# The second product of the last two local chunks in seven-product form for all eight blocks

## The chip, the cores and the metric

The kernel runs on one core of one Trainium2 chip. The metric is device time in microseconds (us) for one execution. A core has five engines that work side by side: TensorE (PE, matrix products), VectorE (DVE), ScalarE (ACT), GpSimd (POOL) and SyncE (SP, which here issues transfers). PE's weight loads are listed apart, as PEld.

## The reference

Eight batches of attention, each with 32 global and 512 local tokens and 8 heads of 64, give a matrix x of 8 x 544 = 4352 rows (one for each token) and 512 columns; two products with a cosine between them follow:

```python
h = x @ w_in                     # 4352 x 512 times 512 x 2048
g = h * np.cos(h)
return (g @ w_out).astype(np.float32)   # w_out: 2048 x 512
```

In the attention every local query sees the 32 global keys and the local keys at a distance of at most 32, and every global query sees all keys.

## The kernel before

**Numbers.** Values are f32. Each operand of a large product is split into two f16 parts, a high and a low one (names end in h and l), and a product is made of three matmuls: high by high, high by low, low by high.

**Tiling.** The tokens are cut into 17 chunks of 256: chunks 0 to 15 are local tokens, two for each batch, and chunk 16 (`NC`) holds the global tokens of all batches. A chunk passes through 8 blocks j, each of 256 of the 2048 columns of w_in. Attention of batch b runs interleaved with the chunks of the batch before, and ends at about 777 us; the chunks after that stand alone. For each block:

- `m1_a` (L1432): 24 matmuls of 256 columns, into the PSUM tile `ph`.
- `m1_b` (ACT L1449, DVE L1450) and `m1_c` (ACT sine, L774): the argument and the cosine, in tile `u`.
- `m1_d`: DVE multiplies (`gf`, L1467), ACT makes the high part (`gh`, L1478), POOL the low part (`gl`, L1479).
- the second product, into two PSUM tiles `po`. In the plain form, `m2_a` (L1585 to L1587), it is 12 matmuls of 512 columns. In the seven-product form it is a 2 x 2 block product after Winograd's scheme: 7 products of a quarter of the size in place of 8. `sv_a` runs four of them (12 matmuls of 256 columns) and `sv_y` three (9 matmuls of 256 columns), all through `three` (L1530). It needs sums of g's quarters, which are made in `m1_d` (four DVE operations on 128x128, L1474 to L1477, with their parts `ygh` on ACT, L1487, and `ygl` on POOL, L1488), and sums of w_out's quarters, which `w_sums` (L1498 to L1513) makes once for each j, around 210 to 250 us.

`seven(c, j)` says which blocks take the seven-product form: those with j of 0 or 1 in chunks 4 to 16, 26 blocks in all. `sv_copy` (L1558, L1560) takes the four quarters of `po` out of PSUM, `m2_b` (L1595, L1605) adds or scales the rest, and `m2_c` (L1622) sends it out.

**Order.** The body lists steps by slot (`at(slot, phase, function, ...)`); `slot0(c)` is the first slot of a chunk. What finally sets the order on each engine is the table `ORDER` (lines 21 to 290): for each engine a list of words `step.instruction`, from which every instruction gets a dependency on the one ahead of it in the table. No engine is free to take another order.

**Names at a place that the change moves.** In attention, `kl` (L917, on DVE) is the low part of a pair's scaled keys and queries, from `qkr` and its high part `qa` (L916, on ACT); `qk_e` moves halves of kh, qa and kl by transfers on SP's queue (L928 to L933), and PE's score matmuls (`ps`, L1184, L1185) need them. `sc_e` copies weights on ACT (`plx`, L1235), takes their low part on POOL (L1237), and a transposing transfer (L1242, `ptb<-plx`) brings them to `av_a` (L1274). `v_q` ends with `vm` (L486) and a PE transpose `pm_v` (L855).

Of the kernel before, what the change touches and what calls it, by code (L numbers as in the profile page):

```python
# [8 lines left out]
F16 = mybir.dt.float16  # L9
# [13 lines left out]
        18x4 22x4 23.4 23.0 23.5 23.1x2 23.6 23.3 23.7 27x4 29.4x3 29.0 29.7 29.1x3 33 33.2 33.1 33.3 35  # L23
        35.4 35.1x3 35.5x3 28x8 34x8 40 40.4 40.1 40.5 40.2 40.6x2 40.3 57 49 69x4 39x8 41x8 74 74.2
        74.1 74.3 64x24 67x24 72x24 108 108.2 108.1 108.3 91x24 106x24 125x24 109 109.4 109.1 109.5
        109.2 109.6 109.3 109.7 135x24 110x2 110.4 110.2 110.5x2 110.3 110.7 124 112x8 113x8 127 127.2
        127.1 127.3 141 141.4x4 141.1x3 143x24 149x8 150 150.4 150.1 150.5 150.2 150.6 150.3 150.7 164x3
        155x5 151x8 152x8 156x20 157x8 164 189x5 164x19 189x3 170x3 170.4 170.3 164 176x22 171x2 189x4
        176x2 187x2 171x18 195x4 196 196.2 196.1 196.3 187x22 206x24 208.6 208.0 208.7 208.1x2 208.8x2
        208.3 208.10 208.4 208.11 208.5 204 209x4 210 210.2 210.1 210.3 227x24 229x2 229.6x2 229.2 229.8  # L30
        229.3x3 229.9x3 250 250.6x3 250.1x2 250.9x2 250.3x3 250.11 274 274.6 274.1x3 274.7x2 274.4 274.9
        274.5 274.10x2 288.6 288.0 288.7 288.1x3 288.8x4 288.4x2 230x18 231x3 231.4x4 231.3 233 233.2
        233.1 233.3 300x2 300.6x3 300.2x2 300.9 300.4x2 300.10 248x24 272x21 234 234.2 234.1 234.3
        230x18 300 303.6 303.0x3 303.7x3 303.3x3 303.10x2 251x2 252x4 272x3 311x12 251x2 253x4 251x32
# [257 lines left out]
P = 128  # L292
# [6 lines left out]
DM = 512  # L299
# [38 lines left out]
T0 = [3, 1]  # L338
# [1576 lines left out]
```

## Time and profile before

| | us |
|---|---|
| median of 3 runs | 927.91 |
| lowest and highest | 926.1, 930.22 |
| the profiled execution's own time | 926.53 |
| its span in the trace | 924.7 |
| PE busy in the span | 876.5 (95%) |
| ACT, DVE, POOL busy | 707.6, 633.4, 511.3 |

The span runs from the first instruction to the last; the 1.8 us between span and time lie outside of it. PE's matmuls are pipelined: the duration printed for one of them is its latency, and what it costs is the distance from its start to the next one's start. The chain of work that ended last, followed back from the end, lies on PE for 56% of the span, on ACT, DVE and POOL for 11% each, and on transfers for 5%.

### The profile page before, as it was taken

How to read it: one execution, taken by the hardware profiler on the slowest of the kernel's cores; microseconds unless marked ns; L12 is line 12 of the kernel's file. 1: busy time of each engine (PE TensorE's matmuls, PEld its weight loads, DVE VectorE, ACT ScalarE, POOL GpSimd, SP SyncE). 2: the span in 40 equal slices, each digit the busy share in tenths (PEclk: the TensorE clock that was granted, in tenths of full speed). 3: DMA queues.
4: the chain of work that ended last, by engine and by line, in shares of the span. 5: the costliest groups of instructions: out<-in, count | busy, mean ns of one | idle time of the engine just before them, and what ended most of it. 6: DMA issues, size and time to landing. Idle time of an engine off the chain costs nothing.

```text
span 924.7 us, 21457 instructions
## 1 busy us (share of the span) xinstructions
PE 876.5 (95%) x8126; PEld 634.2 (69%) x8126; DVE 633.4 (68%) x1684; ACT 707.6 (77%) x1400; POOL 511.3 (55%) x765
## 2 busy tenths in 40 slices
PE   4879888999979999999999999999999999999997
PEld 3668645576756786767777776768686868686853
DVE  6998857599877887787679666778766645451520
ACT  5789998789969889888789798978888856453440
POOL 2577799736727656646565455565655554320340
PEclk9799999999999999999999999999999999999999
DMA  9774516876467666464566654573532524000000
GB/s 359 279 272 162 167 24 148 163 197 153 93 142 146 140 146 113 114 162 92 101 138 157 137 102 102 130 185 77 133 69 51 110 47 84 1 24 1 24 24 23
DMA packets 162423, 110.80 MB, mean 120 GB/s; under 512 B 140176, under 2 KB 142608, under 8 KB 160400
## 3 DMA queue, kind: packets, MB, share of 16 engines
q1 hardware_dynamic: 162176, 109.31, 48.6%
q8 instruction: 63, 1.03, 0.5%
q14 instruction: 40, 0.33, 0.1%
q10 hardware_dynamic: 144, 0.13, 0.1%
HBM read 51.61 MB, written 8.91 MB: 65 GB/s over the span
## 4 chain that ended last, share of the span: by engine, by line
PE 56%; ACT 11%; DVE 11%; POOL 11%; DMA 5%; issue 4%; SPq 1%; DVEq 0%; POOLq 0%; ACTq 0%
PE ph L1432 23%; PE po L1587 7%; PE po L1585 7%; PE po L1586 7%; PE po L1530 4%; DMA ptb<-plx 3%; ACT t L774 2%; PE acc L1274 2%; ACT L774 2%; POOL t L1230 2%; POOL gl L1479 2%; POOL plx L1237 2%; DVE kl L917 1%; POOL plx L819 1%; ACT u L774 1%
## 5 line engine op out<-in xcount | busy, mean ns | idle before, releaser
L1432 PE MATMUL ph<-xh,wi_h 128*128 128x256 f16 x1024 | 280.2, 274 | 4.4 <-DVE gf L1467 4.3
L1432 PE MATMUL ph<-xl,wi_h 128*128 128x256 f16 x1024 | 280.2, 274 | 2.1 <-DVE xl L1110 2.1
L1432 PE MATMUL ph<-xh,wi_l 128*128 128x256 f16 x1024 | 279.4, 274 | 0.2 <-POOL wi_l L516 0.2
L1432 PEld LDWEIGHTS <-wi_h 128*128 128x128 f16 x2176 | 211.5, 98 | 40.0 <-DVE gf L1467 5.1
L1479 POOL TENSOR_TENSOR gl<-gf,gh 128x512 f16<-128x512 f32 x136 | 158.8, 1179 | 129.2 <-ACT gh L1478 113.0
L1586 PE MATMUL po<-wo_l,gh 128*128 128x512 f16 x440 | 161.9, 380 | 0.0
L1585 PE MATMUL po<-wo_h,gh 128*128 128x512 f16 x440 | 157.3, 381 | 0.7 <-DVE o L1605 0.7
L1587 PE MATMUL po<-wo_h,gl 128*128 128x512 f16 x440 | 157.9, 381 | 0.0
L1450 DVE SCALAR_TENSOR_TENSOR u<-ph,ca,u 128x512 f32<-128x512 f32 x136 | 100.5, 743 | 67.5 <-ACT u L1449 67.2
L1230 POOL TENSOR_SCALAR t<-t,sm 128x224 f32<-128x224 f32 (+1 forms) x192 | 83.8, 452 | 111.9 <-DVE sm L1221 64.6
L1449 ACT ACTIVATE u<-ph,quarter,ca 128x512 int32<-128x512 f32 x136 | 104.0, 770 | 54.4 <-PE ph L1432 36.5
L1467 DVE SCALAR_TENSOR_TENSOR gf<-u,ph 128x512 f32<-128x512 f32 x136 | 91.8, 682 | 77.7 <-ACT u L774 57.6
L774 ACT ACTIVATE t<-t,mn 128x224 f32<-128x224 f32 (+1 forms) x256 | 118.2, 463 | 19.7 <-DVE mn L1025 11.6
L1237 POOL TENSOR_TENSOR plx<-t,plx 128x192 f16<-128x192 f32 (+1 forms) x192 | 113.0, 612 | 32.8 <-ACT plx L1235 19.9
L774 ACT ACTIVATE u<-u,halfpi 128x512 f32<-128x512 f32 x136 | 95.9, 718 | 31.7 <-DVE u L1450 30.9
L1432 PEld LDWEIGHTS <-wi_l 128*128 128x128 f16 x1088 | 106.9, 98 | 17.3 <-issue 2.9
L774 ACT ACT_TABLE_LOAD x77 | 98.8, 1283 | 1.2
L1201 DVE CUSTOM_DVE_ANT_0 t<-ps,msk,al 128x192 f32<-128x192 f32 (+1 forms) x192 | 77.5, 426 | 27.9 <-PE ps L1185 27.4
L1478 ACT CAST gh<-gf 128x512 f16<-128x512 f32 x136 | 81.3, 609 | 16.2 <-DVE gf L1467 9.4
L1587 PEld LDWEIGHTS <-gl 128*128 128x128 f16 x440 | 43.1, 98 | 51.2 <-issue 0.7
L1586 PEld LDWEIGHTS <-gh 128*128 128x128 f16 x440 | 43.1, 98 | 46.8 <-issue 1.7
L1585 PEld LDWEIGHTS <-gh 128*128 128x128 f16 x440 | 42.8, 98 | 42.6 <-issue 1.5
(281 smaller groups left out, 1528.4 us busy)
## 6 DMA issues: line engine op xcount, KB each, us to landing
qkr<-qk SPq DMA_DIRECT2D x24, 608.0 KB, 4.7
vr<-v SPq DMA_DIRECT2D x8, 1280.0 KB, 6.0
out<-o SPq DMA_DIRECT2D x33, 256.0 KB, 2.8
kh<-qa SPq DMA_DIRECT2D x48, 152.0 KB, 2.8
wo_h<-wo SPq DMA_DIRECT2D x8, 512.0 KB, 4.5
wo_l<-wo SPq DMA_DIRECT2D x8, 512.0 KB, 3.6
qa<-kl SPq DMA_DIRECT2D x24, 152.0 KB, 2.7
kl<-kl SPq DMA_DIRECT2D x24, 152.0 KB, 2.4
```

The source lines that it names most:

```text
L774: ins = nc.scalar.activation(*a, **k).ins
L1230: nc.gpsimd.tensor_scalar(t[:, h], t[:, h], r[:, h : h + 1], 1.0, op0=ALU.mult, op1=ALU.mult)
L1237: nc.gpsimd.tensor_tensor(lo[:, h], t[:, h], hi[:, h], op=ALU.subtract)
L1432: nc.tensor.matmul((ph.rearrange("p a (k t) -> p a k t", k=2)[:, :, a] if seven(c, j) else ph[:, a]), w[:, kc, f], x[:, kc, q], start=firs ...
L1449: nc.scalar.activation(u.bitcast(I32), ph, AF.Identity, bias=quarter, scale=a)
L1450: nc.vector.scalar_tensor_tensor(u, ph, a, u.bitcast(I32), op0=ALU.mult, op1=ALU.subtract)
L1467: nc.vector.scalar_tensor_tensor(gf, w, 0.25 if c >= CW else 0.5, st.pop(("ph", c, j)).rearrange("p a b -> p (a b)"), op0=ALU.mult, op1=AL ...
L1478: nc.scalar.copy(gh, gf)
L1479: nc.gpsimd.tensor_tensor(gl, gf, gh, op=ALU.subtract)
L1585: nc.tensor.matmul(po[k], gh[:, q], wo_h[:, f], start=(f == first), stop=False, skip_group_check=c >= CW)
L1586: nc.tensor.matmul(po[k], gh[:, q], wo_l[:, f], start=False, stop=False, skip_group_check=c >= CW)
L1587: nc.tensor.matmul(po[k], gl[:, q], wo_h[:, f], start=False, stop=(f == NJ - 1), skip_group_check=c >= CW)
```

## The change

Chunks 14 and 15 (`TL`) take the seven-product form in all eight blocks, so 12 more blocks have it (j from 2 to 7 in two chunks). The sums of w_out that these blocks need, four pairs of high and low part for each j, are made by the new `tail_sums(j)` and lie in tiles that attention used: `plx`, `vhl`, two `qkr` tiles, with the `vr` tile for f32 values. The `y` parts of the new blocks lie in attention's `t` tiles (chunk 14) and in `ptb` and `gpad` (chunk 15). Chunk 15's `po` moves to attention's PSUM. In these two chunks a block's `sv_a` stands one slot after its first product, and all `sv_y` after the chunk's last block. The whole table `ORDER` is new, for all five engines and from the first instruction to the last; of it two lines are shown. Below the old line 620 the changed program's lines are 20 higher up to `m1_d`, and 60 or so higher from `three` on (L1432 becomes L1452, L917 L937, L1530 L1590, L1585 L1646).

```diff
 ORDER = {
     "PE": """
-        18x4 22x4 23.4 23.0 23.5 23.1x2 23.6 23.3 23.7 27x4 29.4x3 29.0 29.7 29.1x3 33 33.2 33.1 33.3 35
...
+        18x4 22x4 23.4 23.0 23.5 23.1x3 23.6x2 27x4 29x3 29.4x3 29.3 29.7 33 33.2 33.1 33.3 28x8 35 35.4
...
+TL = (14, 15)
+TA = 1
...
         def seven(c, j):
-            return c >= CW and j < QS
+            return c in TL or c >= CW and j < QS
...
             if seven(c, j):
-                yh, yl = (
-                    mp2.tile([P, n], F16, tag=t, name=f"y{t}_{c}_{j}", bufs=NG - 4)[:, : 3 * P]
-                    for t in ("gh", "gl")
-                )
+                if j < QS:
...
+                else:
+                    yr = y_room(c, j)
+                    yh, yl = yr[:, :384], yr[:, 384:768]
...
+        def y_room(c, j):
+            if c == TL[0]:
+                t = ap_.tile([P, 2, FW], F32, tag="t", name=f"yt_{c}_{j}", bufs=6)
+                return t.rearrange("p a b -> p (a b)").bitcast(F16)
+            r = ptb.rearrange("p a b c d -> p (a b c d)").bitcast(F16)
+            k = j - QS
+            return gpad[:, : 768] if k == 5 else r[:, 768 * k : 768 * k + 768]
+
+        def tail_rooms():
+            a, b = plx.rearrange("p a b c d -> p (a b c d)"), vhlf
+            q = [t[:, HW * k : HW * k + HW] for t, n in ((a, 16), (b, 20)) for k in range(n)]
+            e = [
+                ap_.tile([P, 2, NZ], F32, tag="qkr", name=f"tr_{k}").rearrange("p a b -> p (a b)").bitcast(F16)
+                for k in range(2)
+            ]
+            f = [t[:, HW * k : HW * k + HW] for t in e for k in range(6)]
+            for k, j in enumerate(range(QS, NS)):
+                tw[j] = [(q[6 * k + 2 * i], q[6 * k + 2 * i + 1]) for i in range(3)] + [(f[2 * k], f[2 * k + 1])]
+            st["tv"] = ap_.tile([P, NPAIR, NT, P], F32, tag="vr", name="tv", bufs=1).rearrange("p a b c -> p (a b c)")
+
+        def tail_sums(j):
+            v = st["tv"][:, 1280 * (j % 2) : 1280 * (j % 2) + 1280]
+            for i in range(2):
+                f = 2 * j + i
+                nc.vector.tensor_tensor(v[:, DM * i : DM * i + DM], wo_h[:, f], wo_l[:, f], op=ALU.add)
+            b11, b12, b21, b22, t3 = (v[:, HW * k : HW * k + HW] for k in range(5))
+            nc.vector.tensor_tensor(t3, b22, b12, op=ALU.subtract)
+            nc.vector.tensor_tensor(b11, b12, b11, op=ALU.subtract)
+            nc.vector.tensor_tensor(b22, b22, b11, op=ALU.subtract)
+            nc.vector.tensor_tensor(b21, b21, b22, op=ALU.subtract)
+            for i, t in enumerate((b11, b21, b22, t3)):
+                h, l = tw[j][i]
+                nc.scalar.copy(h, t)
+                nc.gpsimd.tensor_tensor(l, t, h, op=ALU.subtract)
...
-                    ps.tile([P, DM], F32, tag="po", name=f"po_{c}_{k}", bufs=2) for k in range(CT // P)
+                    ps.tile([P, DM], F32, tag="att", name=f"po_{c}_{k}") if c == TL[1]
+                    else ps.tile([P, DM], F32, tag="po", name=f"po_{c}_{k}", bufs=2) for k in range(CT // P)
...
-                three(c22, sk, wo_q(j, 0, 1))
+                three(c22, sk, wo_q(j, 0, 1) if j < QS else tw[j][3])
...
         def slot0(c):
-            return NS * c + (SH if c > 1 else 0)
+            return NS * c + (SH if c > 1 else 0) + 3 * sum(c > k for k in TL)
...
-                if c >= CW and j < QS:
+                if c in TL:
+                    at(s + TA, m2, sv_a, c, j)
+                    for n, k in enumerate((0, 2, 1)):
+                        at(slot0(c) + NS + TA + (1, 2, 2)[n], PI if k == 1 else m2, sv_y, c, j, k)
+                elif c >= CW and j < QS:
...
+        tl = slot0(TL[0]) + 1
+        at(tl, PA0, tail_rooms)
+        for j in range(QS, NS):
+            at(tl + (j - QS) // 2, PJ, tail_sums, j)
```

In the rows of order below, the last number of a name counts tiles. The numbers ahead of it are the batch and the pair (`kl_3_0`: batch 3, pair 0), for attention's weights also the window (`t_2_2_1`), or the chunk and the block (`gl_2_7`: chunk 2, block 7).

**Place 1: DVE around the low part of batch 3's first pair.** DVE before, at about 248 to 257 us of the trace (`gf_3_1` is block 1 of chunk 3, `vm_3` the scale of batch 3's values):

```order
L846 TENSOR_SCALAR vm_3_3352<-vm_3_3352 128x1
L486 TENSOR_SCALAR qm_3_1_3361<-qm_3_1_3361 128x1
L1467 SCALAR_TENSOR_TENSOR gf_3_1_3433<-u_3_1_3318,ph_3_1_3293 128x512
L1321 COPY gal_3_0_3885<-al_3_0_3072 64x1
L1294 SCALAR_TENSOR_TENSOR xl_2_2845<-acc_2_1_3131,xs_95,xh_2_2844 128x512
L917 SCALAR_TENSOR_TENSOR kl_3_0_3079<-qkr_3_0_2944,qs_3_0_3067,qa_3_0_3078 128x1216
L486 TENSOR_SCALAR vm_3_3352<-vm_3_3352 128x1
L968 TENSOR_REDUCE vs_3_3495<-pm_v3_3482 128x1
```

DVE after, at the same step:

```order
L897 TENSOR_REDUCE qm_3_1_3361<-qkr_3_1_3284 128x1
L866 TENSOR_SCALAR qm_3_1_3361<-qm_3_1_3361 128x1
L1221 ISA t_2_3_1_3347,mn_2_3_1_3348<-ps_2_3_1_3333,msk_73,al_2_3_2911 128x224
L1221 ISA mn_2_3_1_3348 128x1
L1396 TENSOR_SCALAR xg_100<-gacc_2_0_3367,pvs_101 128x64
L937 SCALAR_TENSOR_TENSOR kl_3_0_3079<-qkr_3_0_2944,qs_3_0_3067,qa_3_0_3078 128x1216
L1470 SCALAR_TENSOR_TENSOR u_3_2_3462<-ph_3_2_3437,ca_2_2517,u_3_2_3462 128x512
L1314 SCALAR_TENSOR_TENSOR xl_2_2845<-acc_2_1_3131,xs_95,xh_2_2844 128x512
L1221 ISA t_2_3_2_3507,mn_2_3_2_3508<-ps_2_3_2_3477,msk_73,al_2_3_2911 128x224
```

`xl_2`, which stood ahead of `kl_3_0`, has gone behind it; `xg`, which needs a product of batch 2's global queries, stands ahead of it; and the last row of `vm_3`, which stood right behind it, now stands 23 rows ahead of it.

ACT before, at the same place (`gh_2_6`, `gh_2_7`, `gh_3_0` are high parts; the `plx` rows are the copies of batch 2's weights):

```order
L1235 CAST plx_76<-t_2_2_1_2988 128x2x224
L774 ACTIVATE u_3_1_3318<-u_3_1_3318,halfpi_85 128x512
L1235 CAST plx_76<-t_2_2_2_3074 128x2x224
L1478 CAST gh_2_6_3085<-gf_2_6_3087 128x512
L1235 CAST plx_76<-t_2_2_0_2913 128x2x192
L1235 CAST plx_76<-t_2_2_2_3074 128x2x192
L1293 ACTIVATE xh_2_2844<-acc_2_1_3131,xs_95 128x512
L916 ACTIVATE qa_3_0_3078<-qkr_3_0_2944,qs_3_0_3067 128x1216
L1478 CAST gh_2_7_3189<-gf_2_7_3191 128x512
L1478 CAST gh_3_0_3287<-gf_3_0_3289 128x512
```

ACT after:

```order
L1498 CAST gh_2_6_3085<-gf_2_6_3087 128x512
L1498 CAST gh_2_7_3189<-gf_2_7_3191 128x512
L1498 CAST gh_2_5_3004<-gf_2_5_3006 128x512
L1469 ACTIVATE u_3_1_3318<-ph_3_1_3293,quarter_83,ca_2_2517 128x512
L794 ACTIVATE t_2_3_0_3251,sm_2_3_3625<-t_2_3_0_3251,mn_2_3_0_3252 128x192 x2
L1255 CAST plx_76<-t_2_2_2_3074 128x2x192
L936 ACTIVATE qa_3_0_3078<-qkr_3_0_2944,qs_3_0_3067 128x1216
L1255 CAST plx_76<-t_2_2_0_2913 128x2x192
L794 ACTIVATE gt_2_1_3255,gsm_2_1_3634<-gt_2_1_3255,gmn_2_1_3256 128x544
L1255 CAST plx_76<-t_2_2_1_2988 128x2x224
```

`qa_3_0`, from which `kl_3_0` is made, stood behind four of the `plx` copies and now has two of them behind it; the high parts that stood beside it have gone ahead.

**Place 2: POOL at the same time.** Before:

```order
L1479 TENSOR_TENSOR gl_2_5_3005<-gf_2_5_3006,gh_2_5_3004 128x512
L1237 TENSOR_TENSOR plx_76<-t_2_2_0_2913,plx_76 128x192
L1479 TENSOR_TENSOR gl_2_6_3086<-gf_2_6_3087,gh_2_6_3085 128x512
L1237 TENSOR_TENSOR plx_76<-t_2_2_1_2988,plx_76 128x224
L1237 TENSOR_TENSOR plx_76<-t_2_2_0_2913,plx_76 128x192
L1237 TENSOR_TENSOR plx_76<-t_2_2_2_3074,plx_76 128x224
L1513 TENSOR_TENSOR twwfo_2564<-ws1_1_0_2752,twwfo_2564 128x256
L1237 TENSOR_TENSOR plx_76<-t_2_2_2_3074,plx_76 128x192
L1479 TENSOR_TENSOR gl_2_7_3190<-gf_2_7_3191,gh_2_7_3189 128x512
```

After:

```order
L1257 TENSOR_TENSOR plx_76<-t_2_2_2_3074,plx_76 128x192
L1250 TENSOR_SCALAR t_2_2_1_2988<-t_2_2_1_2988,sm_2_2_3178 128x224
L1499 TENSOR_TENSOR gl_2_6_3086<-gf_2_6_3087,gh_2_6_3085 128x512
L1257 TENSOR_TENSOR plx_76<-t_2_2_1_2988,plx_76 128x224
L1257 TENSOR_TENSOR plx_76<-t_2_2_0_2913,plx_76 128x192 x2
L1257 TENSOR_TENSOR plx_76<-t_2_2_1_2988,plx_76 128x224
L1499 TENSOR_TENSOR gl_2_5_3005<-gf_2_5_3006,gh_2_5_3004 128x512
L1257 TENSOR_TENSOR plx_76<-t_2_2_2_3074,plx_76 128x192
L1499 TENSOR_TENSOR gl_2_7_3190<-gf_2_7_3191,gh_2_7_3189 128x512
```

Before, the DVE operation `kl_3_0` began while POOL was at the last of the three `plx` rows in a row and lasted past the end of these rows; after, the `plx` rows of `t_2_2_0` and `t_2_2_1` stand among POOL's rows, whose ACT copies stand behind `qa_3_0`.

**Place 3: PE at the end.** Before, from the last first-product matmul of chunk 16 (`ph_16_7`) on; behind the last row come the rest of chunk 15's plain matmuls (72 in all) and then chunk 16's:

```order
L1432 LDWEIGHTS wi_l_91
L1432 MATMUL ph_16_7_13143<-xh_g_12755,wi_l_91 128x256
L1530 LDWEIGHTS ygh_15_1_12441
L1530 MATMUL po_15_1_12666<-wo_h_92,ygh_15_1_12441 128x256
L1530 LDWEIGHTS ygh_15_1_12441
L1530 MATMUL po_15_1_12666<-wo_l_93,ygh_15_1_12441 128x256
L1530 LDWEIGHTS ygl_15_1_12442
L1530 MATMUL po_15_1_12666<-wo_h_92,ygl_15_1_12442 128x256
L1585 LDWEIGHTS gh_15_2_12486
L1585 MATMUL po_15_0_12665<-wo_h_92,gh_15_2_12486 128x512
```

After, the last three of the 12 `sv_y` matmuls of chunk 16 that begin right behind `ph_16_7`, and the first of its plain matmuls:

```order
L1590 LDWEIGHTS ygh_16_1_13205
L1590 MATMUL po_16_0_13379<-wo_h_92,ygh_16_1_13205 128x256
L1590 LDWEIGHTS ygh_16_1_13205
L1590 MATMUL po_16_0_13379<-wo_l_93,ygh_16_1_13205 128x256
L1590 LDWEIGHTS ygl_16_1_13206
L1590 MATMUL po_16_0_13379<-wo_h_92,ygl_16_1_13206 128x256
L1646 LDWEIGHTS gh_16_2_13238
L1646 MATMUL po_16_0_13379<-wo_h_92,gh_16_2_13238 128x512
L1646 LDWEIGHTS gh_16_2_13238
L1646 MATMUL po_16_1_13380<-wo_h_92,gh_16_2_13238 128x512
L1647 LDWEIGHTS gh_16_2_13238
L1647 MATMUL po_16_1_13380<-wo_l_93,gh_16_2_13238 128x512
```

Between chunk 16's last first-product matmul and its own plain blocks there stood 72 matmuls of 512 columns of chunk 15 and 45 of 256 columns; now there stand 12 of 256 columns.

## Rows read from the trace of the kernel before

**Rows 1.** The page's part 1: busy time and share of each engine.

```profile
PE 876.5 (95%) x8126; PEld 634.2 (69%) x8126; DVE 633.4 (68%) x1684; ACT 707.6 (77%) x1400; POOL 511.3 (55%) x765
```

**Rows 2.** Stretches: window, length, busy PE, PEld, DVE, ACT, POOL, clock, DMA share, GB/s.

```profile
46.00:275.00 229.00, 206.95 (x1940) 144.57 (x1939) 186.45 (x495) 201.17 (x410) 160.65 (x248) 0.98 0.58 151
...
690.00:775.00 85.00, 84.38 (x836) 60.38 (x834) 49.02 (x131) 60.95 (x124) 45.91 (x68) 1.00 0.45 85
775.00:900.00 125.00, 124.34 (x985) 90.78 (x985) 49.28 (x90) 57.80 (x95) 38.61 (x35) 1.00 0.04 13
```

**Rows 3.** PE's waits from 275 us on: total, times, longest (us).

```profile
PE po L1530 <- DVE o L1595: 1.2, 3, 0.8
```

**Rows 4.** PE's waits from 250 to 270 us.

```profile
PE ps L1185 <- DMA kl<-kl: 2.8, 1, 2.8
PE pm_v L855 <- DVE vm L486: 2.3, 1, 2.3
```

**Rows 5.** The chain that ended last, 815 to 830 us: start, length, what.

```profile
823.55 2.62 PE po L1530 x24
```

**Rows 6.** PE's matmuls in time, 904 to 908 us, first and last of 20 starts.

```profile
904.00 0.38 PE L1585 MATMUL po<-wo_h,gh 128*128 128x512 f16 x1
...
908.10 0.38 PE L1587 MATMUL po<-wo_h,gl 128*128 128x512 f16 x1
```

**Rows 7.** Line 1530's groups: duration in ns (least, median, most), first and last start.

```profile
L1530 PEld LDWEIGHTS <-gh x208: 95/98/98, 329.5 to 900.3; 128*128 128x128 f16 x104
```

**Rows 8.** Groups of side work, in the same columns.

```profile
L1474 DVE TENSOR_TENSOR u<-gf x26: 273/291/1066, 299.5 to 867.6; 128x128 f32<-128x128 f32 x26
...
L1487 ACT CAST ygh<-u x26: 494/504/520, 303.3 to 883.8; 128x384 f16<-128x384 f32 x26
...
L1488 POOL TENSOR_TENSOR ygl<-u,ygh x26: 907/915/1092, 308.9 to 884.9; 128x384 f16<-128x384 f32 x26
...
L1505 DVE TENSOR_TENSOR ws<-wo_h,wo_l x4: 678/683/687, 211.0 to 218.6; 128x512 f32<-128x512 f16 x4
...
L1507 DVE TENSOR_TENSOR ws<-ws x2: 419/422/425, 212.2 to 218.3; 128x256 f32<-128x256 f32 x2
...
L1512 ACT CAST twwlo<-ws x2: 403/404/405, 212.9 to 213.9; 128x256 f16<-128x256 f32 x2
...
L1513 POOL TENSOR_TENSOR twwlo<-ws,twwlo x2: 662/666/670, 214.9 to 216.6; 128x256 f16<-128x256 f32 x2
```

**Rows 9.** PE in time at 775 us; the bracket gives the wait before it.

```profile
775.47 0.61 PE L1274 MATMUL acc<-ptb,vhl 128*64 128x192 f16 x12 [0.61 <-DMA ptb<-plx]
```

**Rows 10.** DVE in time, from 249.67 us.

```profile
249.67 6.54 DVE L917 SCALAR_TENSOR_TENSOR kl<-qkr,qs,qa 128x1216 f16<-128x1216 f32 x1
```

**Rows 11.** Line 917's group: ns (least, median, most).

```profile
L917 DVE SCALAR_TENSOR_TENSOR kl<-qkr,qs,qa x24: 1466/1480/6543, 185.1 to 725.1; 128x1216 f16<-128x1216 f32 x24
```

**Rows 12.** A stretch of that time, in the columns of group 2.

```profile
249.90:254.92 5.02, 4.16 (x39) 3.51 (x37) 5.02 (x1) 4.26 (x12) 5.02 (x7) 1.00 0.02 4
```

**Rows 13.** SP's queue in time, 259 to 264 us.

```profile
259.51 3.90 SPq L1242 DMA_TRANSPOSE ptb<-plx  x2
263.46 0.58 SPq L933 DMA_DIRECT2D kl<-kl  x1
```

**Rows 14.** The page's part 5: groups by line, busy us and mean ns of one.

```profile
L1479 POOL TENSOR_TENSOR gl<-gf,gh 128x512 f16<-128x512 f32 x136 | 158.8, 1179 | 129.2 <-ACT gh L1478 113.0
...
L1450 DVE SCALAR_TENSOR_TENSOR u<-ph,ca,u 128x512 f32<-128x512 f32 x136 | 100.5, 743 | 67.5 <-ACT u L1449 67.2
...
L1449 ACT ACTIVATE u<-ph,quarter,ca 128x512 int32<-128x512 f32 x136 | 104.0, 770 | 54.4 <-PE ph L1432 36.5
L1467 DVE SCALAR_TENSOR_TENSOR gf<-u,ph 128x512 f32<-128x512 f32 x136 | 91.8, 682 | 77.7 <-ACT u L774 57.6
...
L774 ACT ACTIVATE u<-u,halfpi 128x512 f32<-128x512 f32 x136 | 95.9, 718 | 31.7 <-DVE u L1450 30.9
...
L1478 ACT CAST gh<-gf 128x512 f16<-128x512 f32 x136 | 81.3, 609 | 16.2 <-DVE gf L1467 9.4
```

More of the change, by code (lines that the diff above doesn't have):

```diff
@@ new lines @@
+        1156x2 1156.2x4 1171 1171.6 1171.1x2 1171.7x2 1171.3x3 1171.9x3 1181x4 1169 1192x8 1177x21 1179
+        1179.6x5 1179.1 1179.11 1179.2x4 1194 1194.6x3 1194.1x3 1194.9x2 1194.4x2 1194.11 1213x24
+        1199x36 1200x4 1233x24 1215x2 1215.3x3 1215.2 1215.9x3 1215.6x3 1216.3x2 1216.0 1216.5x2
+        1216.1x2 1216.9x3 1216.7x2 1220x4 1221x8 1222 1253x24 1240x4 1235x3 1237x3 1241x8 1245x60
+        1267x24 1284x6 1257x4 1236x3 1247x2 1284x18 1247 1270x36 1271x4 1248x3 1238x3 1255x3 1255.6x3
@@ new lines @@
+        1493x24 1459x36 1460x4 1475x7 1475.9x3 1475.7x2 1476.3x2 1476.0x3 1476.5x2 1476.9x3 1476.7x2
+        1513x24 1480x4 1481x8 1482 1495x3 1497x2 1527x24 1544x24 1500x4 1501x8 1505x60 1496x3 1561x8
+        1517x4 1498x2 1497 1561x16 1507x3 1508x3 1498 1569x15 1515x3 1515.6x6 1515.3x3 1530x36 1531x4
+        1547 1584x24 1529.6x2 1529.0x2 1529.8x2 1529.2x4 1529.10x2 1548x2 1549 1548x2 1569x9 1564x4
+        1546.6x4 1573x4 1546 1546.0 1546.11 1546.1x5 1563.6 1563.0x5 1563.7x2 1563.5 1563.9x3 1571x4
@@ new lines @@
+        1571.6x2 1571.4 1571.8x2 1571.5 1571.10x2 1604x24 1586.6 1586.0x4 1586.7x4 1586.4x2 1586.11
+        1590x36 1624x3 1591x4 1644x24 1624x21 1606x7 1606.9x3 1606.7x2 1611x4 1658x24 1612x8 1613
+        1607.3x3 1607.0 1607.6 1607.1x2 1607.9 1607.7x2 1607.10x2 1631x4 1632x8 1636x60 1626x3 1627x3
+        1648x4 1628x3 1674x7 1629x3 1689x24 1674x17 1697x8 1638x3 1639x3 1697x15 1661x36 1662x4 1646.6
+        1646.0 1646.7x3 1646.1x3 1646.10 1646.4x2 1646.11 1660.6 1660.0 1660.7x4 1660.1x2 1660.11
@@ L290 @@
+        1599 1578 1601 1600 1655 1651 1649 1650 1652 1647.1 1647.0 1654 1671 1700x2 1708 1702 1726 1706
+        1703 1725 1727 1704 1705 1771 1772 1773 1774 1811 1810 1812 1813 1814 1825 1826 1897 1896 1950
+        1951 2024 2025 2073 2081
     """,
@@ L1481, in m1_d @@
             if seven(c, j):
-                yh, yl = (
-                    mp2.tile([P, n], F16, tag=t, name=f"y{t}_{c}_{j}", bufs=NG - 4)[:, : 3 * P]
-                    for t in ("gh", "gl")
-                )
+                if j < QS:
+                    yh, yl = (
+                        mp2.tile([P, n], F16, tag=t, name=f"y{t}_{c}_{j}", bufs=NG - 4)[:, : 3 * P]
+                        for t in ("gh", "gl")
+                    )
+                else:
+                    yr = y_room(c, j)
+                    yh, yl = yr[:, :384], yr[:, 384:768]
                 sf = w[:, : 3 * P]
@@ L1806, in body @@
                 at(m - 1, ob, chunk_out_scale, c)
-                w = m + (QS + 1) // 2
+                w = slot0(c) + NS + TA + 1 if c in TL else m + (QS + 1) // 2
                 at(w - 1, ob, sv_out, c)
@@ L1810, in body @@
                 at(w - 1, ob, sv_copy, c, 3, 1)
[L1811 to L1812 removed]
+                at(w + (c in TL), ob, sv_copy, c, 1, 3)
+                at(w + (c in TL), PJ, sv_copy, c, 2, 3)
             else:
@@ L1816, in body @@
                 e = k * (NS - QS) if c == NC else 0
-                at(m + NS - 1 + e, ob, m2_b, c, k)
-                at(m + NS + e, oc, m2_c, c, k)
+                n = slot0(c) + NS + TA + 3 if c in TL else m + NS - 1 + e
+                at(n, ob, m2_b, c, k)
+                at(n + 1, oc, m2_c, c, k)
+        tl = slot0(TL[0]) + 1
+        at(tl, PA0, tail_rooms)
+        for j in range(QS, NS):
+            at(tl + (j - QS) // 2, PJ, tail_sums, j)
         at(TS0, PA0, w_rooms)
```

486 lines of the change are left out of this document (241 added, 245 removed), and 32 rows, old and new, of the table ORDER.

## The prediction

> **What bounds the kernel now.** I read the busy shares first, then PE's busy time stretch by stretch, then PE's waits, and last the distance between matmul starts. PE is busy for 876.5 of 924.7 us, and no other engine comes above 77% [rows 1]. From 690 to 775 us PE does 84.38 of 85 us and from 775 to 900 us 124.34 of 125 [rows 2]. There the time is the number of matmuls times their distance, and only fewer or cheaper matmuls, or one of the few waits, can change it. Between 46 and 275 us PE is idle for 229.00 - 206.95 = 22.05 us [rows 2]; there the order of the work counts. The other engines have room where the change adds work: from 775 to 900 us DVE, ACT and POOL are idle for 75.7, 67.2 and 86.4 us, from 690 to 775 us for 36.0, 24.1 and 39.1 us (length less busy time) [rows 2].
>
> **Term 1, the matmuls.** The duration printed for a matmul is latency, so I take distances. 24 matmuls of 256 columns of the seven-product form in a row take 2.62 us on the chain, 0.1092 us each [rows 5]. Twenty starts of 512-column matmuls span 4.10 us, 19 steps of 0.2158 us [rows 6]. A plain block is 12 x 0.2158 = 2.590 us, a seven-product block 21 x 0.1092 = 2.293 us. Twelve blocks change: 12 x (2.293 - 2.590) = **-3.56 us**, all of it on PE, and PE is the bound there. The first product of these blocks writes its tile in another layout, but keeps its 24 matmuls: nothing.
>
> The new weights for PE could cost something: 252 weight loads come for 144. A load of this form takes 0.098 us [rows 7], and the 0.1092 us above is the distance with such a load ahead of every matmul, so it lies beside the matmul before it. The Trainium skill says otherwise (TensorE: Matmul & The Clock Gate, Part 3, The mechanism): a weight load overlaps a running matmul only where the row groups differ, which is never so here. By that rule the term would be rival E's instead of -3.56 us; the distances of [rows 5, 6] contradict it, since they leave no room for a load beside the columns.
>
> **Term 2, the added side work.** Each new block adds four DVE sums of 0.29, a copy on ACT of 0.50 and a difference on POOL of 0.92 us [rows 8]: over 12 blocks 13.9, 6.0 and 11.0 us. The sums of w_out add for each of six j two DVE additions of 0.683 and four subtractions of 0.422 (6 x 3.05 = 18.3 us), four copies on ACT of 0.40 (9.7 us) and four differences on POOL of 0.67 us (16 us) [rows 8]. The table of after puts the sums of j = 2 and 3 among chunk 12's work, j = 4 and 5 among chunk 13's, 6 and 7 among chunk 14's, so all lie between about 690 us and the end, where the idle times above exceed the whole (DVE 32 of 111.7, ACT 16 of 91, POOL 27 of 125). I cost them at nothing; PE's matmuls hide them. Without that cover one held operation costs about what the worst one of before lost, 5 us (term 4).
>
> The second product of these two chunks comes sooner after the first. The way from a block's last first-product matmul to its low part is 0.77 + 0.74 + 0.72 + 0.68 + 0.61 + 1.18 = 4.70 us [rows 14], with two to four sums of 0.29 us about 5.9 us. By the new table at least 12 us of PE work lie between the two in chunk 15, and at least 18 in chunk 14 (over 36 before, counted with the distances above). In chunk 16's last block it is 12 x 0.109 + 31 x 0.216 = 8.0 us, so about 2 us are to spare. Nothing again, with up to 2 us if ACT's queue holds a step there.
>
> **Term 3, small waits at the tail.** The last attention product waits 0.61 us for a transpose at 775 us [rows 9]. Between its last scores and itself stood 91 matmuls of 256 and 48 of 512 columns, 20.3 us; now it is 117 and 72, 28.3 us. The wait goes: **-0.6 us**. Seven-product matmuls wait 1.2 us for the last addition of the chunk before [rows 3]; chunk 15 now has PSUM of its own, which takes some of that away, and the quarter copies in three chunks may bring as much. I take 0, with -1.2 and +1.2 as ends.
>
> **Term 4, the collision at 250 us.** The low part `kl` of batch 3's first pair took 6.54 us on DVE [rows 10], where its group's median is 1.48 [rows 11]: 5.06 us lost. In those 5.02 us POOL ran seven operations without a gap, DVE just the one, and PE fell to 4.16 us [rows 12]. Behind `kl` on DVE stood `vm`, for which PE then waited 2.3 us; for `kl` itself, whose second transfer was issued at 263.46 behind transposes of 3.90 us [rows 13], it waited 2.8 us [rows 4]. The Trainium skill has this mechanism (SBUF - State Buffer, Who interferes with whom): a DVE operation with two inputs in SBUF and a GpSimd operation that reads SBUF exclude each other; the row of 6.54 us agrees with it.
>
> In the new table `vm` stands 23 rows ahead of `kl`, so its wait goes: **-2.3 us**, unless `kl` is held as before and the next row behind it is late in its place. Whether it is held: POOL's run needs ACT's copies of the weights, and two of these now stand behind `qa`, of which `kl` is made; and `xg`, which waits for PE, stands ahead of `kl`. So POOL should pause for ACT about when `kl` starts. Against it: the same kinds of rows still stand on POOL, and its backlog may be long enough. I hold it for three to two that `kl` isn't held for long. The 2.8 us of the transfer go only if the transposes ahead of it do not wait for something else: 0 to -2.8, and I take 0, since a transpose still stands between the two transfers.
>
> **The sum.** The profiled execution took 926.53 us, 1.83 beside its span; nothing of the change touches what lies outside the span. 926.53 - 3.56 - 0.61 - 2.3 = 920.1 us. The median of the runs is 1.38 us above the profiled one, so 921.4 us.
>
> **The rivals.** A difference of 0.5% is 4.6 us, about what a measurement of this kernel can tell from no change: below 923.3 is faster, above 932.5 slower.
>
> *A, the forecast:* tail gain, and the collision is mostly gone. 921.4 us; 918.6 if the transfer's wait goes too, and 917.4 with the 1.2 us of term 3.
>
> *B, only the tail:* `kl` is held as before, and whatever stands behind it (chunk 3's argument `u`) is late in place of `vm`. 927.91 - 3.56 - 0.61 = 923.7 us. For it: two-input DVE operations and POOL's weights still share this stretch. Against it: the two points on ACT and DVE above.
>
> *C, the gain is given back ahead of the tail:* every instruction has moved, and in the 229 us from 46 on, PE is already idle for 22 us [rows 2]. A few transfers or low parts that arrive later than now would cost 2 to 5 us over B: 925.7 to 928.7 us, about 927.
>
> *D, slower:* the change adds 84 DVE operations with two SBUF inputs (48 sums of g, 36 of w_out). If a run on POOL holds such an operation as it held `kl`, with PE's next argument queued behind it, each case costs up to 5.06 us. Two such places on top of B give 923.7 + 10.1 = 933.8 us, and it decides from 8.8 us of new waits on. For it: the longest of 26 such sums took 1.07 us where 0.29 is usual [rows 8]. Against it: even that one lost under 1 us, and PE has over 12 us in hand there.
>
> *E, the matmuls cost more:* the weight loads of the twelve blocks lie bare ahead of their matmuls, in both forms. A block then goes from 12 x (0.2158 + 0.098) = 3.77 to 21 x (0.1092 + 0.098) = 4.35 us, twelve blocks add 7.0 us, and the time is 927.91 + 7.0 - 0.6 - 2.3 = 932.0 us. The distances speak against it [rows 5 to 7]: they are those of a stream with a load for each matmul. The rule of the Trainium skill named in term 1 speaks for it; the trace disagrees.
>
> **How the numbers follow.** A 0.46, B 0.32, C 0.12, D 0.08, E 0.02. Faster by over 0.5%: A, and an eighth of B, 0.50. Within 0.5%: the rest of B, C, and E's lower half, 0.41. Slower: D and E's upper half, 0.09. The range takes all of A and B and half of C, 917.4 to 927.0 us; A's own is 917.4 to 923.3.
>
> **What would show it.** Of the changed kernel: after the last attention product a stretch with PE busy above 99%, 21 matmuls at distances of 0.109 us in the new blocks, and 144 long matmuls fewer. The row of `kl` after: 1.5 us is A, over 4 us is B. No wait of `pm_v` for `vm`, and none before the last attention product. I am wrong in term 2 if PE waits for `gl`, `ygl` or a sum of w_out after 690 us; in term 4 if `kl` is short but PE's waits between 46 and 275 us still add up to 22 us.

## The result, and the profile after

The changed kernel takes 913.62 us (median of 4 runs, 913.16 to 913.74), before 927.23 us (926.1 to 930.22): a ratio of 0.9845 with an interval of 0.9821 to 0.9868. That is 13.6 us less, where 6.5 had been forecast, and 3.8 us below the range. The profiled execution took 913.73 us, with a span of 911.4. Its first part, in the columns of [rows 1]:

```profile
PE 868.9 (95%) x8234; PEld 641.6 (70%) x8234; DVE 666.3 (73%) x1768; ACT 724.8 (80%) x1442; POOL 542.9 (60%) x801
```

DVE, ACT and POOL are busy for 32.9, 17.2 and 31.6 us more, where term 2 had 32, 16 and 27 us, and PE for 7.6 us less.

**The tail.** Both kernels from the end of the same amount of earlier work to the last matmul, first before, then after, in the columns of [rows 2]:

```profile
770.20:919.10 148.90, 147.49 (x1140) 104.00 (x1137) 53.05 (x98) 62.04 (x103) 39.77 (x36) 1.00 0.07 21
```
```profile
762.20:906.10 143.90, 143.53 (x1242) 113.83 (x1240) 77.88 (x164) 72.02 (x131) 60.46 (x63) 1.00 0.05 17
```

PE's busy time falls by 3.96 us although 102 matmuls more are recorded, and its idle time from 1.41 to 0.37 us. The waits of before in that stretch were 0.6 us for the transpose of [rows 9] and these two:

```profile
PE po L1530 <- ACT o L1558: 0.6, 1, 0.6
PE po L1530 <- DVE o L1595: 0.2, 1, 0.2
```

All that PE still waits for after, from 700 us on (the second lies ahead of 762 us):

```profile
PE ph L1452 <- DVE gf L1487: 0.4, 1, 0.4
PE po L1646 <- ACT o L1619: 0.4, 1, 0.4
```

On the chain that ended last, 36 seven-product matmuls of new blocks in a row, read as in [rows 5]; some of them read the new sums of w_out in `plx`:

```profile
820.29 3.93 PE po L1590 x36
```

They are 0.1092 us apart, to the digit as before, with a weight load ahead of each.

**The collision.** DVE and POOL around batch 3's `kl`, to be read against [rows 10] and [rows 12]:

```profile
245.81 1.47 DVE L937 SCALAR_TENSOR_TENSOR kl<-qkr,qs,qa 128x1216 f16<-128x1216 f32 x1
```
```profile
244.63 1.17 POOL L1499 TENSOR_TENSOR gl<-gf,gh 128x512 f16<-128x512 f32 x1
246.03 3.30 POOL L1257 TENSOR_TENSOR plx<-t,plx 128x224 f16<-128x224 f32 x4 [0.23 <-ACT plx L1255]
```

`kl` took 1.47 us in place of 6.54. It began as POOL's `gl` ended, and POOL then waited 0.23 us for ACT's copy of the weights. The first of POOL's four `plx` rows took 1.72 us, the longest of the four, where their median is 0.58: here POOL was the one held, until `kl` had ended. From 205 to 290 us PE waits for one thing only, where [rows 4] had 2.3 and 2.8 us:

```profile
PE ph L1452 <- DVE qs L880: 0.5, 1, 0.5
```

**Where the 13 us lie.** To compare the traces stage by stage although the order differs, each matmul is counted at the median distance of its form in the traces of before and after; this sum is the work done (837 us before, 833.4 after). The table gives the time that each stretch of this work took, in us, up to the end of the last matmul. A few such tables stand below for the other kernels; their stretches are the same.

| work done, us | before | before, second trace | after | after, second trace |
|---|---|---|---|---|
| 0 to 55 | 90.3 | 90.7 | 91.1 | 92.2 |
| 55 to 110 | 71.4 | 69.8 | 67.8 | 68.5 |
| 110 to 190 | 87.1 | 87.4 | 88.5 | 88.6 |
| 190 to 215 (the collision) | 30.7 | 31.3 | 25.6 | 25.6 |
| 215 to 340 | 130.7 | 129.7 | 128.6 | 128.8 |
| 340 to 480 | 144.0 | 144.0 | 144.0 | 144.4 |
| 480 to 690 | 216.0 | 215.3 | 216.7 | 216.9 |
| 690 to the end (the tail) | 148.9 | 148.8 | 143.9 | 143.9 |
| all | 919.1 | 917.0 | 906.1 | 908.5 |

The collision's stretch gives 5.1 us, the tail 5.0, the stretches of 55 to 110 and 215 to 340 another 3.6 and 2.1, and 0 to 55, 110 to 190 and 480 to 690 take 0.8, 1.4 and 0.7 back. Up to 190 us of work the four columns add up to 248.8, 247.9, 247.4 and 249.3 us: the gain of 55 to 110 leaves nothing net there, since two traces of one kernel differ by as much.

### The profile page after: what moved, and what is told of

It reads as the page before. It is cut to its first block, busy times and chain, and to the rows that moved or that the text cites. A ratio compares the mean times of both kernels' runs of the same rounds, so it can differ in the third digit from the quotient of the medians.

```text
span 911.4 us, 21837 instructions
## 1 busy us (share of the span) xinstructions
PE 868.9 (95%) x8234; PEld 641.6 (70%) x8234; DVE 666.3 (73%) x1768; ACT 724.8 (80%) x1442; POOL 542.9 (60%) x801
## 5 line engine op out<-in xcount | busy, mean ns | idle before, releaser
L1452 PE MATMUL ph<-xh,wi_h 128*128 128x256 f16 x1024 | 280.3, 274 | 3.6 <-DVE gf L1487 2.8
L1452 PE MATMUL ph<-xl,wi_h 128*128 128x256 f16 x1024 | 279.6, 274 | 1.3 <-DVE xl L1130 1.0
L1452 PE MATMUL ph<-xh,wi_l 128*128 128x256 f16 x1024 | 279.3, 273 | 0.0
L1452 PEld LDWEIGHTS <-wi_h 128*128 128x128 f16 x2176 | 211.2, 98 | 39.7 <-issue 4.6
L1250 POOL TENSOR_SCALAR t<-t,sm 128x224 f32<-128x224 f32 (+1 forms) x192 | 85.9, 464 | 112.1 <-DVE sm L1241 81.9
L1647 PE MATMUL po<-wo_l,gh 128*128 128x512 f16 x392 | 143.4, 381 | 1.8 <-POOL wo_l L536 1.8
L1648 PE MATMUL po<-wo_h,gl 128*128 128x512 f16 x392 | 141.6, 381 | 1.6 <-POOL gl L1499 1.5
L1646 PE MATMUL po<-wo_h,gh 128*128 128x512 f16 x392 | 139.9, 380 | 0.5 <-ACT o L1619 0.5
L1257 POOL TENSOR_TENSOR plx<-t,plx 128x192 f16<-128x192 f32 (+1 forms) x192 | 111.6, 605 | 37.6 <-ACT plx L1255 31.9
L1452 PEld LDWEIGHTS <-wi_l 128*128 128x128 f16 x1088 | 106.6, 98 | 14.7 <-issue 0.9
L1648 PEld LDWEIGHTS <-gl 128*128 128x128 f16 x392 | 38.4, 98 | 48.5 <-POOL gl L1499 3.1
L1647 PEld LDWEIGHTS <-gh 128*128 128x128 f16 x392 | 38.4, 98 | 42.7 <-issue 2.6
L1646 PEld LDWEIGHTS <-gh 128*128 128x128 f16 x392 | 38.0, 98 | 38.5 <-issue 2.3
```

What stands on the lines that cost most here:

```text
L1250: nc.gpsimd.tensor_scalar(t[:, h], t[:, h], r[:, h : h + 1], 1.0, op0=ALU.mult, op1=ALU.mult)
L1257: nc.gpsimd.tensor_tensor(lo[:, h], t[:, h], hi[:, h], op=ALU.subtract)
L1452: nc.tensor.matmul((ph.rearrange("p a (k t) -> p a k t", k=2)[:, :, a] if seven(c, j) else ph[:, a]), w[:, kc, f], x[:, kc, q], start=firs ...
L1646: nc.tensor.matmul(po[k], gh[:, q], wo_h[:, f], start=(f == first), stop=False, skip_group_check=c >= CW)
L1647: nc.tensor.matmul(po[k], gh[:, q], wo_l[:, f], start=False, stop=False, skip_group_check=c >= CW)
L1648: nc.tensor.matmul(po[k], gl[:, q], wo_h[:, f], start=False, stop=(f == NJ - 1), skip_group_check=c >= CW)
```

## The experiments

**The early order alone, and the tail alone.** A table of the order can be put together from two: first, on each engine, all that had started by some time in one kernel's trace, in its order, then the rest in the other kernel's. Two kernels take the changed order for the early part and keep plain products, two the reverse.

```diff
 # e1_early (the changed order up to 300 us) and e2_early (up to 494 us), on the kernel before
     "PE": """
-        18x4 22x4 23.4 23.0 23.5 23.1x2 23.6 23.3 23.7 27x4 29.4x3 29.0 29.7 29.1x3 33 33.2 33.1 33.3 35
...
+        18x4 22x4 23.4 23.0 23.5 23.1x3 23.6x2 27x4 29x3 29.4x3 29.3 29.7 33 33.2 33.1 33.3 28x8 35
...
 # e1_tail (the order of before up to 620 us) and e2_tail (up to 500 us), on the changed kernel
-        18x4 22x4 23.4 23.0 23.5 23.1x3 23.6x2 27x4 29x3 29.4x3 29.3 29.7 33 33.2 33.1 33.3 28x8 35 35.4
...
+        18x4 22x4 23.4 23.0 23.5 23.1x2 23.6 23.3 23.7 27x4 29.4x3 29.0 29.7 29.1x3 33 33.2 33.1
...
```

> The kernel before, with its plain products in the last chunks, but on every engine the instructions that had started by 300 us in the trace of the changed kernel come first, in the changed kernel's order; behind them the order of before. Theory (two thirds of the gain lie ahead of the tail, most of it in the order between 240 and 300 us): about 920.5 us, 6.7 less than before. Rival (the gain is in the new form of the last chunks and what comes with it): 927, no change.

> The changed kernel, but everything that had started by 620 us in the trace of before stands first, in the order of before; behind it the changed kernel's order with the new form in chunks 14 and 15. Theory: the form's 3.6 us of matmuls and some 1 us of waits, about 922.6 us. Rival (the new form brings all of the gain): about 914.

> As the run that put the order of before first up to 620 us, with the seam at 500 us, where the two orders stand nearly alike. Theory: the new form's 3.6 us and about 1 us of waits at the tail show without a loss at the seam: about 4.6 us under before, 923. Rival (the new form gives only what the first such run showed, and the rest of the gain is elsewhere): 926.

> The kernel before with plain products in the last chunks, with everything that had started by 494 us in the trace of the changed kernel first, in its order. Theory (waits of 290 to 420 us add some 1.5 us to the gain ahead of 300): about 917. Rival (the gain ahead of the tail is all in the stretch to 300 us): 918.4, as with the seam at 300.

Measured: e1_early 918.37 us (917.56 to 921.4), 0.9907 of before (0.9879 to 0.9936); e1_tail 926.28 (0.9961 to 0.9998); e2_tail 923.98 (0.9949 to 0.9983); e2_early 923.05 (0.9944 to 0.9974). By the stretches:

| work done, us | before | e1_early | e2_early | e1_tail | e2_tail | after |
|---|---|---|---|---|---|---|
| 0 to 55 | 90.3 | 94.5 | 94.3 | 91.1 | 90.4 | 91.1 |
| 55 to 110 | 71.4 | 68.5 | 69.2 | 69.7 | 68.9 | 67.8 |
| 110 to 190 | 87.1 | 88.5 | 86.8 | 87.2 | 87.9 | 88.5 |
| 190 to 215 | 30.7 | 25.6 | 25.6 | 33.1 | 31.2 | 25.6 |
| 215 to 340 | 130.7 | 129.7 | 128.6 | 130.6 | 129.8 | 128.6 |
| 340 to 480 | 144.0 | 144.3 | 147.2 | 144.0 | 143.4 | 144.0 |
| 480 to 690 | 216.0 | 214.8 | 214.9 | 219.7 | 216.8 | 216.7 |
| 690 to the end | 148.9 | 148.4 | 149.0 | 144.1 | 144.4 | 143.9 |

The tail's stretch falls by 4.5 to 5.0 us wherever the new form is there, and by 0.5 at most where it isn't; the collision's falls by 5.1 us wherever the changed order is there. So the two halves of the gain are separate and add up. Up to 190 us of work the tables' kernels with the order of before take 247.2 to 248.8 us, those with the changed order 247.4 to 251.5: there the new order gains nothing. The medians of three of the four are off what was expected. e1_tail is 3.7 us over, and the stretch with its seam at 620 us is 3.7 us longer than before; e2_early is some 6 us over, with 3.2 us at its seam at 494 us and 4.0 us ahead of 55. e1_early came 2.1 us under; its trace is that of its slowest run (921.4 us), so the 4.2 us that it shows ahead of 55 (below) need not be in its median. The rival that the new form alone brings all of the gain is out. In 215 to 340 e2_early takes 128.6 us as after does, e1_early 129.7; with the order of before the tables have 129.7 to 130.7.

**What held `kl`.** One dependency is added to the kernel before: step 392 is the sum of w_out whose low part stood at the start of [rows 12].

```diff
+        tc.add_manual_dep([i for i in steps[392] if i.engine == E_.Pool][2], st["klins", 12].name, sync, reason="kl ahead")
         for name, line in ORDER.items():
```

> The kernel before with one dependency more: the POOL operation that stood at 249.9 us (the low part of a sum of w_out) waits until the low part kl of batch 3's first pair is done on DVE. Theory (POOL's unbroken run holds kl, and both waits of PE, 2.3 and 2.8 us, come from that): kl takes 1.5 to 2 us, both waits go, about 922.1 us. Rival (only the first wait comes from kl; the transfer is late because of the transposes ahead of it): about 924.9. Rival (kl is slow for another reason): 927 and kl still over 6 us.

Measured: 920.6 us (920.21 to 921.43), 0.9927 of before (0.9903 to 0.9951). DVE and POOL in its trace:

```profile
249.99 1.56 DVE L917 SCALAR_TENSOR_TENSOR kl<-qkr,qs,qa 128x1216 f16<-128x1216 f32 x1
251.47 0.14 DVE L486 TENSOR_SCALAR vm<-vm 128x1 uint32<-128x1 uint32 x1
```
```profile
248.59 1.68 POOL L1237 TENSOR_TENSOR plx<-t,plx 128x224 f16<-128x224 f32 x3
251.62 0.67 POOL L1513 TENSOR_TENSOR twwfo<-ws,twwfo 128x256 f16<-128x256 f32 x1 [1.36 <-DVE vm L486]
```

POOL pauses for 1.36 us, `kl` takes 1.56, and from 245 to 275 us PE waits for nothing. The stretch of 190 to 215 falls from 30.7 to 25.4 us, the others stay as before: 5.3 us from one pause of POOL. Both waits of [rows 4] hang on `kl`, the transfer's too. SP's queue shows why, before and then with the pause:

```profile
256.28 0.46 SPq L931 DMA_DIRECT2D qa<-kl  x1
```
```profile
251.62 0.46 SPq L931 DMA_DIRECT2D qa<-kl  x1
258.52 0.58 SPq L933 DMA_DIRECT2D kl<-kl  x1
```

The first transfer of `kl` stands ahead of the transposes of [rows 13] on that queue. When it comes 4.7 us earlier, the transposes do too, and the second transfer is issued at 258.52 in place of 263.46.

This one dependency also does as much for PE between 46 and 275 us as the whole new table. With it, and then after, in the columns of [rows 2]:

```profile
46.00:275.00 229.00, 213.24 (x1978) 148.86 (x1978) 183.10 (x501) 205.48 (x425) 165.30 (x256) 0.97 0.58 154
```
```profile
46.00:275.00 229.00, 212.77 (x1983) 148.23 (x1982) 185.74 (x499) 210.84 (x430) 170.07 (x261) 0.98 0.60 156
```

PE idles for 15.76 and 16.23 us there, against 22.05 before.

**Only `vm` moved.** In DVE's table the word of `vm` (489) goes ahead of that of `kl` (447).

```diff
-490 496 578 457 447 489 508x2 508.3 498
+490 496 578 457 489 447 508x2 508.3 498
```

> The kernel before with one row of DVE moved: the last row of vm, the scale of batch 3's values, stands ahead of kl and not behind it. The prediction's step: the wait of 2.3 us goes although kl is still held, about 924.9 us. Rival (what stands next behind kl is late in place of vm): no change, 927, with PE waiting as long for something else.

Measured: 925.85 us, 0.9991 of before (0.9969 to 1.0013). `kl` still takes 6.49 us, and PE waits for two things from 245 to 275 us:

```profile
PE ps L1196 <- DMA kl<-kl: 3.2, 1, 3.2
PE ph L1443 <- DVE gf L1478: 1.5, 1, 1.5
```

The wait for `vm` is gone, and one for `gf`, queued behind `kl`, stands in its place; the stretch takes 31.9 us against 30.7 and 31.3 in the two traces of before. The times alone do not decide between the two forecasts, since the interval reaches from 2.9 us faster to 1.2 slower; the stretch does, for the rival: in that trace the move gives nothing there.

**Whether the tail's side work is free.** Parts of the new sums of w_out are made twice, each copy right behind the first: on all three engines (e2_side), and on one at a time.

```diff
 # e3_dve
+                for _ in range(2):
                     nc.vector.tensor_tensor(v[:, DM * i : DM * i + DM], wo_h[:, f], wo_l[:, f], op=ALU.add)
...
+            for _ in range(2):
                 nc.vector.tensor_tensor(t3, b22, b12, op=ALU.subtract)
 # e3_act
+                for _ in range(2):
                     nc.scalar.copy(h, t)
 # e3_pool
+                for _ in range(2):
                     nc.gpsimd.tensor_tensor(l, t, h, op=ALU.subtract)
```

> The changed kernel, with half of the DVE operations (both additions and the first subtraction) and all ACT copies and POOL subtractions of the new sums of w_out made twice: 10.7 us more on DVE, 9.7 on ACT, 16 on POOL from 690 us on. Theory (PE's matmuls hide the side work): the same time, 913.6 to 914.6. Rival (the side work is at its limit there and is part of the price): 917 or more, with PE waiting for low parts or for sums.

> The changed kernel with only POOL's subtractions of the new sums of w_out made twice, 16 us more on POOL. Theory (POOL is the thin cover: the next sum on DVE waits until POOL has read the last one, and chunk work is queued behind it on DVE): most of the 28 us that doubling on three engines cost, 930 or more, with DVE's tv waiting for POOL. Rival (no single engine is the limit, only their sum): under 920.

> The changed kernel with only the two additions and the first subtraction of each new sum of w_out made twice on DVE, 10.7 us more on DVE. Theory (POOL is the thin cover): 914 to 917. Rival (DVE is): 925 or more.

> The changed kernel with only ACT's copies of the new sums of w_out made twice, 9.7 us more on ACT. Theory (POOL is the thin cover): 914 to 917. Rival (ACT is, since POOL's subtractions wait for these copies): 925 or more.

Measured: 941.78 us for all three, 924.26 for POOL, 927.76 for DVE, 919.79 for ACT. By the stretches of 480 to 690 and 690 to the end:

| | after | e3_act | e3_pool | e3_dve | e2_side |
|---|---|---|---|---|---|
| added work, us | | 9.7 | 16 | 10.7 | 36 |
| 480 to 690 | 216.7 | 216.8 | 216.7 | 219.9 | 219.9 |
| 690 to the end | 143.9 | 148.2 | 152.5 | 150.0 | 165.9 |
| more than after | | 4.4 | 8.6 | 9.3 | 25.2 |

Both theories fall: the added side work is not hidden, and POOL is no single thin cover. POOL's run and ACT's came out between their two forecasts, DVE's at its rival's. Every engine's added work costs about half of itself or more, and the three add up to 22.3 of the 25.2 us. The trace of e2_side shows how. From 759 to 769 and from 769 to 779 us, in the columns of [rows 2]:

```profile
759.00:769.00 10.00, 10.00 (x71) 6.49 (x70) 6.04 (x6) 3.66 (x9) 9.61 (x12) 1.00 0.09 18
769.00:779.00 10.00, 2.98 (x100) 2.73 (x100) 8.41 (x18) 2.49 (x5) 1.69 (x3) 0.79 0.10 18
```

POOL and then DVE in that time:

```profile
759.47 6.41 POOL L1591 TENSOR_TENSOR plx<-tv,plx 128x256 f16<-128x256 f32 x8
```
```profile
762.30 2.22 DVE L1579 TENSOR_TENSOR tv<-wo_h,wo_l 128x512 f32<-128x512 f16 x2 [3.82 <-POOL plx L1591]
...
770.80 1.42 DVE L1579 TENSOR_TENSOR tv<-wo_h,wo_l 128x512 f32<-128x512 f16 x2 [1.32 <-POOL plx L1591]
...
777.67 0.74 DVE L1672 SCALAR_TENSOR_TENSOR o<-po,co,o 128x512 f32<-128x512 f32 x1
```

The next sum on DVE writes the tile `tv` that POOL has still to read, so DVE waits for POOL; behind it in DVE's fixed order stand the addition that frees `po` (L1672) and the next argument, and PE gets 2.98 us of 10 done.

**The scatter.** Two kernels were run and traced a second time.

> The kernel before once more, for a second trace. Its times spread over 8 us, those of the kernels in which kl is not held over about 1. Theory (what varies from run to run is the hold of DVE by POOL): in a trace of another time, kl is longer or shorter than 6.5 us by the difference, or another DVE operation is held. Rival (the spread arises in the first 50 us, in the loads): kl 6.5 us again, with the difference ahead of 60 us.

> The changed kernel once more, for a second trace and its scatter beside that of before. Theory (what spreads the times of before is in its order, the hold of kl and the first 60 us; the changed order has none of it): 913 to 914.5 us, spread of about 1 us. Rival (the spread is the chip's): a spread of several us here too.

Measured: before 924.47 us in that one run, with `kl` at 6.56 us again, so its hold did not vary; the 2.1 us by which the second trace is shorter lie in 55 to 110, 215 to 340 and 480 to 690, so neither forecast holds. After 915.48 us (912.82 to 917.21), so its times spread too. In the traces of all kernels the stretches behind 110 repeat within about 2 us, apart from the edits and seams. The first 55 us of work take 89.6 to 95.5 us; the largest is 95.5, of e3_dve, whose order there is the changed kernel's. From 46 to 100 us, in the columns of [rows 2], after, e1_early and e3_dve:

```profile
46.00:100.00 54.00, 47.12 (x446) 37.55 (x445) 47.70 (x118) 49.37 (x93) 40.31 (x59) 0.97 0.56 185
```
```profile
46.00:100.00 54.00, 49.75 (x440) 39.57 (x440) 45.50 (x114) 47.76 (x95) 39.28 (x56) 0.88 0.49 171
```
```profile
46.00:100.00 54.00, 49.70 (x438) 39.20 (x437) 45.71 (x115) 47.17 (x93) 39.47 (x57) 0.87 0.50 165
```

The slow starts have PE busier with fewer matmuls at a granted clock of 0.87 and 0.88, where 0.97 stands in the first and 0.95 in the second trace of after (means over the stretch of the two levels, 2.4 and 1.2 GHz). In all four, PE is busy for only 27 to 28 of the 46 us ahead of it. So clock and time go together here; which of them brings the other, and what decides it in a run, was not tried.

## Why the prediction missed

**What bounds, and term 1: right.** PE sets the time from 275 us on. The term of -3.56 us came out as -3.64 by the counted work and -3.96 by PE's busy time; 0.1092 us holds in the new blocks, and the weight loads stay beside the matmuls, so rival E is out. The Trainium skill's rule weighed there (TensorE: Matmul & The Clock Gate, Part 3, The mechanism) disagrees with this trace once more.

**Term 2: about right in its result, wrong in its reason.** From 690 us of work on PE idles for 0.37 us, so the side work there costs next to nothing as it stands. Some of the sums lie ahead of that: 480 to 690 took 0.7 us longer (up to 1.6 between the other pairs of traces), and whether they are the cause was not tried. But the prediction argued from average idle shares (32 of 111.7 us on DVE and so on), and the doubled sums show that such idle time is not room. DVE, ACT and POOL wait for each other and for PE there, and what is put into a fixed order delays all that is queued behind it. 10.7 us more on DVE alone cost 9.3 us, more than the 5.0 that the tail gains. The places that the table gives the sums may be why they came out cheap; no run moved them.

**Term 3: undersized.** 0.6 us was forecast; the tail's idle time fell by 1.04 us. The transpose's 0.6 went as said. Of the 1.2 us of [rows 3], which the term counted to the tail, only 0.2 lies there, and 1.0 at 340 to 410 us. The term had no place for the 0.6 us that PE waited for ACT's copy out of `po`, which went too; one new wait, 0.4 us for `gf`, came.

**Term 4: the step that failed.** The mechanism was right: POOL's unbroken run, a pause for ACT's copies when `kl` starts, and `kl` at 1.47 us. That it came out so was held for only three to two, and the pause was short, 0.23 us. The size was not right. The step took 2.3 us for `vm` and put the transfer's 2.8 us at 0, "since a transpose still stands between the two transfers". It overlooked that these transposes themselves stood behind the first transfer of `kl`. The added pause of POOL took both waits away with the order of the queue as it was, 5.3 us; in the changed kernel the stretch fell by 5.1. And moving `vm` ahead, which the sum rested on, gave nothing in the stretch of e1_vm; it was the freed DVE that counted. The 5.06 us that the row of `kl` was too long would have been close to both.

**What had no term.** The prediction treated the rest of the new table only as a danger (rival C) and never as a gain. In 215 to 340 it gained 2.1 us (0.9 to 1.9 between the other pairs of traces): the two waits that before had there, 1.0 us for the addition that frees `po` and 0.6 for transposes, are gone. The 3.6 us of 55 to 110 are not shown to be the table's: with the order of before that stretch takes 68.9 to 71.4 us, with the changed order 67.8 to 69.2, and up to 190 us of work nothing is left of it. An estimate: the time of e1_gap less the tail's gain, 920.6 - 5.0 = 915.6 us, is what one dependency in the old order and the new form might give together, beside medians of 913.62 and 915.48 for the changed kernel; no run has both.

**The sum.** Up to the last matmul the trace is 13.0 us shorter, -5.0 for the tail, -5.1 for the collision and net -2.8 for the rest but for rounding, where the terms had -6.5. Of the 6.5 us missing, 2.8 are term 4's, 0.8 lie in the tail (half in waits, half in PE's busy time) and 2.8 in the rest, much of which is no more than what two traces of one kernel differ by. The 1.38 us by which the median of before stood above its profiled run were carried over to the forecast; after's median lies at its own profiled run. That made the forecast 1.4 us later; where in the runs the 1.38 us arose is not shown. The four together are the 7.8 us from 921.4 to 913.6.

None of the other rivals came. No run found a time under the changed kernel's: the splices of both orders lose at their seams or keep the collision.

## What to carry to other kernels

An operation several times as long as its group's median on a busy engine can be worth its whole excess, as here (5.1 to 5.3 us for 5.06), if all that PE waits for behind it hangs on it: look for it in the least, median and most of each group, and break the other engine's run with one dependency before reordering anything. Follow the queue that its result goes through as well: a transfer that seems to stand behind other work comes sooner if that work too stands behind the result. Idle shares of in-order engines that wait for each other are no room: double the work to see what it costs before counting it at nothing. And when a whole table of the order is new, give its untouched stretches a range on both sides, from the idle time that PE has in each; and take a second trace of both kernels before a difference of one or two us in a stretch is put down to the order.

## What the hardware showed

The hold of `kl` was 6.5 us in all five traces that had it (6.49 to 6.56 us), since POOL had seven operations in a row ready: it did not give way between two of them. The Trainium skill (SBUF - State Buffer, Who interferes with whom) has the exclusion of a two-input DVE operation and a GpSimd one that reads SBUF, which this trace agrees with; that a whole run of them counts, not one, is what the rows add. With the run broken once, POOL lost 1.36 us and PE gained 5.3; in the changed kernel, where `kl` got in first, it was POOL's operation that took 1.72 us.

The other thing was the granted clock from 46 to 100 us: with equal orders it was 0.87 to 0.97 there, and in the traces with 0.87 and 0.88 the first 55 us of work took 94.5 and 95.5 us, where those with 0.95 and 0.97 took 92.2 and 91.1. That goes with nearly as much time as the new form brings; which is the cause was not tried.
